# A four-block transformer stack on one core: left-over queries copied beside a segment's own, the output projection in halves of heads and columns, and a new table of order

## The chip, the cores and the metric

The kernel runs on one core of a Trainium2 chip. A core has five engines with instruction streams of their own: TensorE (PE in the profile; its weight loads are listed apart as PEld), VectorE (DVE), ScalarE (ACT), GpSimd (POOL) and SyncE (SP). They meet only through semaphores and share one on-chip memory; products land in eight accumulation banks (pb0 to pb7, 128 partitions by 512 floats), from which DVE or ACT must copy them out. The metric is the device time of one execution in microseconds; lower is better.

## The reference

`x` is 2048 tokens by 512. Four residual blocks follow each other: A, B, A, B, each on a layernorm of `x`.

```python
def _A_ref(x, mem0, Wq, Wk, Wv, Wo, seg_len):      # 32 heads of 128, M = 8 memory rows, seg_len = 32
    mem = mem0
    for s in range(n_seg):                          # 64 segments, one after the other
        h = concat([mem, x[32 rows of segment s]])  # 40 rows
        q, k, v = h @ Wq, h @ Wk, h @ Wv
        scores = where(mask, q @ k.T * scale, -1e9) # memory columns open to all, the rest causal
        o = softmax(scores) @ v @ Wo
        mem = o[:8]                                 # the next segment's memory
        outs.append(o[8:])

def _B_ref(x, wqkv, wo):                            # linear attention, 32 heads of 16
    pq, pk = phi(q), phi(k)                         # phi(t) = t+1 or exp(t), plus 1e-6
    kv = sum over tokens of pk^T v;  z = sum of pk
    o = (pq @ kv) / (pq . z + 1e-6);  return o @ wo
```

Block A is a recurrence over 64 segments: a segment's first eight output rows enter the next one's projections. Two A blocks make 128 such steps.

## The kernel before

**Rows.** A segment with its memory has 40 rows, but the column-tiled products take 32. So a block of 32 rows holds the eight memory rows (places 0 to 7) and the first 24 tokens (8 to 31). The left-over eight tokens of four segments form a fifth block of 32 rows, the left block, projected once for four segments (`prepare`, `left_block`). 128 tokens, four segments, are a tile; there are 16.

**A segment.** `project` (L721) multiplies a block with Wq, Wk and Wv. Four products of 32 output rows each go to the four 32-column groups of the array (`tile_position`), group j taking heads 8j to 8j+7; a run of 16 products fills a bank with half of the heads (half b = 0 or 1). Q and K are then turned: the bank is copied out (L572 on ACT, L573 on DVE), and half 0 is transposed by a DMA on SP's queue (L734), half 1 by TensorE (L741) and another copy. Results are `qT`, `kT`, and `qTl`, `kTl` of the left block.

**Memory attention** (`mem_attention`, L802 to L836) handles the eight memory queries: the products with left keys and own keys, exp, mask, sums, reciprocal by Ln and Exp, product with V, and a multiplication into `oTb`. **Own attention** (`x_attention`, L854 to L893) takes the 24 own queries and the eight left-over ones of the segment against the own keys: for each of the 32 heads one product with `qT[..., 8:32]` (24 columns, L854) and one with `qTl` (8 columns, L856), under the same keys. Its results are used one segment later.

**Output.** `out_proj` (L913) runs 32 products of 512 columns, column group j again holding heads 8j to 8j+7, so the bank holds four partial sums over heads in four row groups. Two copies of 256 columns bring it to `outW`. `next_mem` (L936) picks rows 0 to 7 and adds the four partial sums with `selm`, four products with `outW` as weights; a small copy puts the result into the next block. `residual` (L951, L956) picks the other rows with `selx` and `sell` as weights and 512 moving columns. `outW` and these selectors are 32-bit.

**Block B** is worked per tile of 128 tokens: `b_in` (L1045 to L1081) behind the A block's last rows, `b_mid` once, `b_out` (L1137, L1147) before the next A block's tile or at the end. Weights are loaded at the start: Wv, Wk and Wq by DMAs on ACT's queue, Wo in four parts and wqkv on SP's, and B's `wo` on POOL's.

**Order.** A planner (`_Prog`) sets each engine's order at build time. Every operation has a place (segment, name of its group, number in it); its priority is segment times `PERIOD` plus an entry of `OFFSET`, lower first, among what the planner's own costs make ready. `MODE_SLACK` says how long TensorE may prefer work of the same mode, column-tiled or whole array. The program that comes out is a fixed sequence for each engine with semaphore waits.

## Time and profile before

| | |
|---|---|
| median of three runs | 1967.08 us (1965.83 to 1967.78) |
| the profiled execution | 1967.05 us, span 1965.3 us |
| mean granted TensorE clock | 0.990 |
| busy: PE, ACT, DVE | 93%, 66%, 49% of the span |
| products and weight loads recorded | 39757 and 39837 |
| DMA | 96.31 MB |

The profile names a group of instructions by source line, engine, operation and tiles, with its count, the time in which at least one of them ran, the mean of one, and the engine's idle time just before them with what ended it. A product's duration contains the time in which it drains, during which the next one already runs; how far apart products start is therefore read from the starts in the timeline. Nearly all small tiles lie in one allocation, `arena_sb`.

### The profile page before, as it was taken

How to read it: one execution, taken by the hardware profiler on the slowest of the kernel's cores; microseconds unless marked ns; L12 is line 12 of the kernel's file. 1: busy time of each engine (PE TensorE's matmuls, PEld its weight loads, DVE VectorE, ACT ScalarE, POOL GpSimd, SP SyncE). 2: the span in 40 equal slices, each digit the busy share in tenths (PEclk: the TensorE clock that was granted, in tenths of full speed). 3: DMA queues.
4: the chain of work that ended last, by engine and by line, in shares of the span. 5: the costliest groups of instructions: out<-in, count | busy, mean ns of one | idle time of the engine just before them, and what ended most of it. 6: DMA issues, size and time to landing. Idle time of an engine off the chain costs nothing.

```text
span 1965.3 us, 86728 instructions
## 1 busy us (share of the span) xinstructions
PE 1836.8 (93%) x39757; PEld 1108.9 (56%) x39837; DVE 960.1 (49%) x2856; ACT 1295.4 (66%) x3170; POOL 74.5 (4%) x172
## 2 busy tenths in 40 slices
PE   2899999999999999999789999999999999999996
PEld 0455565556555655656445566555656556665652
DVE  1254455455445545454544455555455455555555
ACT  1566666666676766766456767666767777776765
POOL 2000000000000000000000000000000000000000
PEclk9899999999999999999899999999999999999999
DMA  8511222122112211211121211211122121222213
GB/s 307 123 32 35 40 38 43 32 38 38 38 35 37 43 32 42 34 40 35 28 43 27 40 40 40 38 35 43 35 40 46 33 43 38 40 38 41 55 35 118
DMA packets 228221, 96.31 MB, mean 49 GB/s; under 512 B 211624, under 2 KB 222000, under 8 KB 226320
## 3 DMA queue, kind: packets, MB, share of 16 engines
q1 hardware_dynamic: 220656, 62.58, 17.5%
q0 software_dynamic: 5616, 15.60, 2.6%
q10 hardware_dynamic: 1584, 12.58, 1.6%
q8 instruction: 311, 5.10, 1.1%
q14 instruction: 54, 0.44, 0.1%
HBM read 29.89 MB, written 10.49 MB: 21 GB/s over the span
## 4 chain that ended last, share of the span: by engine, by line
PE 80%; DMA 14%; ACT 3%; DVE 2%; issue 1%; ACTq 0%; SPq 0%; DVEq 0%
PE pb L721 33%; PE pb L913 15%; DMA arena_sb<-arena_sb 11%; PE pb L892 3%; PE pb L802 3%; PE pb L936 3%; PE pb L854 3%; PE pb L741 3%; PE pb L1045 3%; PE pb L819 2%; PE pb L951 2%; DMA Wq_sb<-in_A_Wq_dram 2%; ACT arena_sb L572 2%; PE pb L1081 1%; PE pb L833 1%; PE pb L832 1%
## 5 line engine op out<-in xcount | busy, mean ns | idle before, releaser
L572 ACT ACTIVATE arena_sb<-pb 128x512 bf16<-128x512 f32 (+5 forms) x1448 | 749.9, 525 | 385.5 <-PE pb L721 288.3
L721 PE MATMUL pb<-Wq_sb,arena_sb 128*32 128x512 bf16 x5120 | 342.8, 384 | 20.8 <-DMA Wq_sb<-in_A_Wq_dram 20.5
L721 PE MATMUL pb<-Wk_sb,arena_sb 128*32 128x512 bf16 x5120 | 339.2, 381 | 0.0
L721 PE MATMUL pb<-Wv_sb,arena_sb 128*32 128x512 bf16 x5120 | 330.1, 381 | 0.3 <-DVE arena_sb L573 0.3
L913 PE MATMUL pb<-Wo_sb,arena_sb 128*32 128x512 bf16 x5184 | 320.6, 384 | 3.7 <-DMA Wo_sb<-in_A_Wo_dram 2.8
L573 DVE COPY arena_sb<-pb 128x512 bf16<-128x512 bf16 (+2 forms) x356 | 123.1, 362 | 279.2 <-PE pb L741 275.2
L877 DVE TENSOR_TENSOR arena_sb<-arena_sb 32x256 bf16<-32x256 bf16 x512 | 212.7, 415 | 70.3 <-ACT arena_sb L873 58.4
L572 ACT ACTIVATE outW_sb<-pb 128x256 fp32r<-128x256 f32 x290 | 111.4, 384 | 162.7 <-PE pb L913 157.9
L721 PEld LDWEIGHTS pb<-Wv_sb,arena_sb 128*32 128x32 bf16 x5120 | 143.3, 97 | 133.5 <-issue 2.6
L721 PEld LDWEIGHTS pb<-Wk_sb,arena_sb 128*32 128x32 bf16 x5120 | 137.7, 97 | 134.5 <-issue 1.6
L721 PEld LDWEIGHTS pb<-Wq_sb,arena_sb 128*32 128x32 bf16 x5120 | 128.1, 97 | 146.8 <-DMA Wq_sb<-in_A_Wq_dram 20.8
L913 PEld LDWEIGHTS pb<-Wo_sb,arena_sb 128*32 128x32 bf16 x5184 | 138.2, 97 | 115.0 <-issue 5.9
L573 DVE CAST arena_sb<-pb 128x128 bf16<-128x128 f32 (+3 forms) x282 | 101.0, 358 | 202.7 <-PE pb L721 62.8
L892 PE MATMUL pb<-arena_sb 128*128 128x128 bf16 x1024 | 139.5, 218 | 5.1 <-DVE arena_sb L879 5.1
L893 PE MATMUL pb<-arena_sb 128*128 128x32 bf16 x1024 | 126.7, 179 | 0.0
L802 PE MATMUL pb<-arena_sb 128*128 128x32 bf16 x2016 | 108.0, 177 | 17.4 <-DMA arena_sb<-arena_sb 15.5
L809 ACT ACTIVATE arena_sb<-pb 128x256 bf16<-128x256 f32 x252 | 96.1, 382 | 38.7 <-PE pb L802 30.7
L879 DVE TENSOR_TENSOR arena_sb<-arena_sb 32x64 bf16<-32x64 bf16 x512 | 111.0, 217 | 15.8
L741 PE MATMUL pb<-id_sb,arena_sb 128*128 128x128 bf16 x1024 | 86.1, 221 | 25.3 <-ACT arena_sb L572 20.7
L741 PEld LDWEIGHTS pb<-id_sb,arena_sb 128*128 128x128 bf16 x1024 | 57.7, 98 | 86.2 <-ACT arena_sb L572 52.6
L802 PEld LDWEIGHTS pb<-arena_sb 128*128 128x128 bf16 x2016 | 84.4, 96 | 24.7 <-DMA arena_sb<-arena_sb 18.3
L892 PEld LDWEIGHTS pb<-arena_sb 128*128 128x128 bf16 x1024 | 91.3, 97 | 6.6 <-DVE arena_sb L879 5.7
(109 smaller groups left out, 2406.7 us busy)
## 6 DMA issues: line engine op xcount, KB each, us to landing
arena_sb<-arena_sb SPq DMA_TRANSPOSE x384, 2.5
Wv_sb<-in_A_Wv_dram ACTq DMA_DIRECT2D x1, 4096.0 KB, 15.0
Wk_sb<-in_A_Wk_dram ACTq DMA_DIRECT2D x1, 4096.0 KB, 24.9
Wq_sb<-in_A_Wq_dram ACTq DMA_DIRECT2D x1, 4096.0 KB, 34.2
Wo_sb<-in_A_Wo_dram SPq DMA_DIRECT2D x4, 1024.0 KB, 7.1
xs_scratch<-x_sb POOLq DMA_DIRECT2D x32, 128.0 KB, 2.0
pq_scratch<-arena_sb POOLq DMA_DIRECT2D x32, 128.0 KB, 3.1
x_sb<-xs_scratch POOLq DMA_DIRECT2D x16, 128.0 KB, 2.3
```

The costliest lines, as they stand in the source:

```text
L572: return e.activation(o() if callable(o) else o, i() if callable(i) else i, ACTF.Copy)
L573: return e.tensor_copy(o() if callable(o) else o, i() if callable(i) else i)
L721: r = pe.matmul(tl.f32()[32 * j:32 * j + 32, 0:512], blk[:, c, :], W[:, c, o:o + 512], start=(c == 0), stop=(c == 3), tile_position=(0, 32 ...
L741: r = pe.transpose(tt.bf16()[:, 128 * i:128 * i + 128], img[:, k, 128 * i:128 * i + 128], id_sb[:, :])
L802: r = pe.matmul(tl.f32()[:, o:o + 32], kk[:, hh, :, :].rearrange("p j x -> p (j x)"), qT[:, r2, hh, :, 0:8], start=True, stop=True)
L809: add("act", lambda a: a.activation(Pm[:, k, :, :].rearrange("p a q -> p (a q)"), tl.f32()[:, 0:256], ACTF.Exp, scale=SCALE), c_act(256), ...
L854: pe.matmul(tl.f32()[q, 32 * hh:32 * hh + 24], kT[:, r2, hh, j, :], qT[:, r2, hh, j, 8:32], start=True, stop=True, tile_position=(0, 32 * j))
L877: add("dve", lambda v, q=q, j=j: v.tensor_tensor(Pbx[q, :, j, 0:32], Px[q, :, :], Rx[q, :, :], ALU.mult), c_dve(256) + 0.075, reads=["Px", ...
L879: add("dve", lambda v, q=q, j=j: v.tensor_tensor(Pbx[q, :, j, 32:40], PLL[q, g2, :, gl], Rx[q, :, 24:32], ALU.mult), c_dve(64) + 0.075, re ...
L892: pe.matmul(o, vimg[:, r2, e], Pbx[:, hh, :, 0:32], start=True, stop=False)
L893: return pe.matmul(o[:, :, 24:32], vleft[:, g2, e], Pbx[:, hh, :, 32:40], start=False, stop=True)
L913: r = pe.matmul(tl.f32()[32 * j:32 * j + 32, :], oT[:, 4 * hh + j, :], Wo_sb[:, 8 * j + hh, :], start=(hh == 0), stop=(hh == 7), tile_posi ...
```

## The change

1. In `x_attention` the eight left-over queries of the segment are copied from `qTl` into `qT[..., 0:8]`, over the memory queries, one copy for each half of heads; then a single product of 32 columns per head takes the place of the 24 and 8. The left-over queries now stand at 0 to 7 instead of 24 to 31, and the slices behind follow (sums, multiplications, products with V, copies, and the mask `mx`).
2. In `out_proj` a column group holds half of the heads and half of the columns: 64 products of 256 columns. The bank then holds two partial sums of heads by two column halves in 256 columns. The two copies are 128 columns wide. `next_mem` has two products, each with a 16-column selector for both column halves; `residual` has two products of 256 columns with different selectors for one of 512.
3. The loads get places in the table (`ld0` to `ld4`), the load of B's `wo` waits until wqkv has landed, and the memory load is listed ahead of the first `x` load.
4. `OFFSET` is a new table, with groups of their own for the first and last tiles; `MODE_SLACK` goes from 25.37 to 26.39 and `LOOK` from 0.103 to 0.

```diff
-MODE_SLACK = 25.37
-LOOK = 0.103
+MODE_SLACK = 26.39
+LOOK = 0.000
...
+    "ld2": (20.70,),
+    "ld3": (4.75,),
+    "ld4": (-15.85,),
...
+    for i, (W, v, nm, t) in enumerate(((Wq_sb, qk_view[0], "Wq", 12.0), (Wk_sb, qk_view[1], "Wk", 21.0),
+                                       (Wv_sb, qk_view[2], "Wv", 30.3))):
+        P.at(-998 + i, "ld%d" % (2 + i))
+        late.append(add("act", lambda a, W=W, v=v: a.dma_start(W[:, :, :], v), 0.5, writes=[nm], dsem="d" + nm, lat=t))
...
     def load_wo_b(n):
-        add("pool", lambda e: e.dma_start(MB_sb[:, :, :], B_wo.rearrange("(c p) f -> p c f", p=128)), 1.1,
+        add("pool", lambda e: e.dma_start(MB_sb[:, :, :], B_wo.rearrange("(c p) f -> p c f", p=128)), 1.1, after=[late[-1]],
...
+            for b in range(2):
+                hs = slice(4 * b, 4 * b + 4)
+                evac(qT[:, r2, hs, :, 0:8], qTl[:, g2, hs, :, gl], 128, reads=[("qTl", g2, b)], writes=[("qT", r2, b)])
...
                         for j in range(4):
-                            q = slice(32 * j, 32 * j + 32)
-                            pe.matmul(tl.f32()[q, 32 * hh:32 * hh + 24], kT[:, r2, hh, j, :], qT[:, r2, hh, j, 8:32],
-                                      start=True, stop=True, tile_position=(0, 32 * j))
-                            r = pe.matmul(tl.f32()[q, 32 * hh + 24:32 * hh + 32], kT[:, r2, hh, j, :],
-                                          qTl[:, g2, hh, j, gl], start=True, stop=True, tile_position=(0, 32 * j))
+                            r = pe.matmul(tl.f32()[32 * j:32 * j + 32, 32 * hh:32 * hh + 32], kT[:, r2, hh, j, :],
+                                          qT[:, r2, hh, j, :], start=True, stop=True, tile_position=(0, 32 * j))
...
                 def mm(pe, hh=hh):
-                    for j in range(4):
-                        r = pe.matmul(tl.f32()[32 * j:32 * j + 32, :], oT[:, 4 * hh + j, :], Wo_sb[:, 8 * j + hh, :],
-                                      start=(hh == 0), stop=(hh == 7), tile_position=(0, 32 * j))
+                    for i in range(2):
+                        for j in range(4):
+                            k, d = divmod(j, 2)
+                            n = 2 * k + i
+                            r = pe.matmul(tl.f32()[32 * j:32 * j + 32, 0:256], oT[:, 4 * hh + n, :],
+                                          Wo_sb[:, 8 * n + hh, 256 * d:256 * d + 256], start=(hh == 0 and i == 0),
+                                          stop=(hh == 7 and i == 1), tile_position=(0, 32 * j))
...
-                cs = slice(256 * h, 256 * h + 256)
-                evac(outW[:, w, cs], lambda cs=cs: tl.f32()[:, cs], 256, tiles=[tl],
+                cs = slice(128 * h, 128 * h + 128)
+                evac(outW[:, w, cs], lambda cs=cs: tl.f32()[:, cs], 128, tiles=[tl],
...
-                    for c in (2 * h, 2 * h + 1):
-                        r = pe.matmul(tl.f32()[:, 8 * c:8 * c + 8], outW[:, w, 128 * c:128 * c + 128], selm_sb[:, :],
-                                      start=True, stop=True)
+                    return pe.matmul(tl.f32()[:, 16 * h:16 * h + 16], outW[:, w, 128 * h:128 * h + 128], selm_sb[:, :],
+                                     start=True, stop=True)
...
+            def pick(pe, sel, u, first, last):
+                for d in range(2):
+                    r = pe.matmul(tl.f32()[:, 256 * d:256 * d + 256], sel(d), outW[:, u, :], start=first and d == 0, stop=last,
+                                  skip_group_check=True)
+                return r
```

Since the table decides the order, three places of the built programs are shown. The first is ACT's stream at the start of the program, with the three large weight loads; before:

```order
L600 DMA Wv_sb<-in_A_Wv_dram 128x4x4096
L600 DMA Wk_sb<-in_A_Wk_dram 128x4x4096
L600 DMA Wq_sb<-in_A_Wq_dram 128x4x4096
L615 ACT_TABLE_LOAD
L572 ACTIVATE memT_sb<-pb 128x32
```

and in the changed program:

```order
L624 DMA Wv_sb<-in_A_Wv_dram 128x4x4096
L624 DMA Wk_sb<-in_A_Wk_dram 128x4x4096
L624 DMA Wq_sb<-in_A_Wq_dram 128x4x4096
L640 ACT_TABLE_LOAD
L591 ACTIVATE memT_sb<-pb 128x32
```

The three loads stand in the same order in both: V's weights first, Q's last.

The second place is TensorE's stream in the second segment of a tile (segment 17 of the first A block), from the projection of K's half 0, which a DMA turns, to the memory attention's products (L802, L834 after). Lines L721 and L753 are projections, L741 and L773 TensorE's transposes of half 1; the bank numbers are shown. Before:

```order
L721 MATMUL pb4<-Wk_sb,arena_sb 32x512 x16
L721 MATMUL pb1<-Wq_sb,arena_sb 32x512 x16
L721 MATMUL pb7<-Wv_sb,arena_sb 32x512 x16
L721 MATMUL pb2<-Wk_sb,arena_sb 32x512 x16
L721 MATMUL pb6<-Wv_sb,arena_sb 32x512 x16
L741 MATMUL pb5<-id_sb,arena_sb 128x128 x4
L741 MATMUL pb3<-id_sb,arena_sb 128x128 x4
L802 MATMUL pb4<-arena_sb 128x32 x8
```

and in the changed program:

```order
L753 MATMUL pb6<-Wk_sb,arena_sb 32x512 x16
L753 MATMUL pb1<-Wk_sb,arena_sb 32x512 x16
L753 MATMUL pb7<-Wq_sb,arena_sb 32x512 x16
L753 MATMUL pb4<-Wv_sb,arena_sb 32x512 x16
L753 MATMUL pb3<-Wv_sb,arena_sb 32x512 x16
L773 MATMUL pb2<-id_sb,arena_sb 128x128 x4
L834 MATMUL pb0<-arena_sb 128x32 x4
L773 MATMUL pb5<-id_sb,arena_sb 128x128 x4
L925 MATMUL pb6<-arena_sb 128x128
L926 MATMUL pb6<-arena_sb 128x4x8
```

Half 1 of Q and K now goes ahead of both projections of V, and the two transposes are set apart, with four memory products between them; a further pair of L925 and L926 with its like, four transposes of a layernorm and then the second four memory products (which wait for K's DMA) follow.

The third is TensorE's stream in the same kind of segment, from the output projection (L913, L949 after) to the next segment's first projection. L868 and L869 are the own attention's sums, L1045 and L1085 products of block B, L889 the own scores. Before:

```order
L913 MATMUL pb1<-Wo_sb,arena_sb 32x512 x32
L868 MATMUL pb3<-arena_sb,bo_sb 128x256
L869 MATMUL pb3<-arena_sb,bo_sb 128x8x8
L951 MATMUL pb0<-outW_sb,selx_sb 128x512
L956 MATMUL pb0<-outW_sb,sell_sb 128x512
L936 MATMUL pb4<-selm_sb,outW_sb 128x8 x4
L951 MATMUL pb2<-outW_sb,selx_sb 128x512
L721 MATMUL pb7<-Wq_sb,arena_sb 32x512 x16
```

and in the changed program:

```order
L949 MATMUL pb0<-Wo_sb,arena_sb 32x256 x64
L889 MATMUL pb4<-arena_sb 32x32 x32
L753 MATMUL pb2<-Wv_sb,arena_sb 32x512 x16
L753 MATMUL pb7<-Wq_sb,arena_sb 32x512 x16
L972 MATMUL pb1<-selm_sb,outW_sb 128x16 x2
L1085 MATMUL pb6<-arena_sb 128x512 x2
L901 MATMUL pb4<-arena_sb,bo_sb 128x256
L902 MATMUL pb4<-arena_sb,bo_sb 128x8x8
L753 MATMUL pb5<-Wq_sb,arena_sb 32x512 x16
```

The own scores now follow the output projection instead of going ahead of it, two projections of the left block stand between the output projection and the memory products, and B's products and the sums stand between these and the next projection. Over the whole program TensorE changes between column-tiled and whole-array products 586 times before and 654 times now.

133 lines of the change are left out of this document (77 added, 56 removed), and 8 rows, old and new, of the table OFFSET.

## The prediction

> **What bounds the kernel now.** I read the page's totals and slices first.
>
> ```profile
> span 1965.3 us, 86728 instructions
> PE 1836.8 (93%) x39757; PEld 1108.9 (56%) x39837; DVE 960.1 (49%) x2856; ACT 1295.4 (66%) x3170; POOL 74.5 (4%) x172
> PE   2899999999999999999789999999999999999996
> ```
>
> TensorE is busy from the second slice to the last, with one dip where the second A block begins. A busy PE may still be a waiting one, so the busy time by stages came next (columns: length, then busy time and count of each engine).
>
> ```profile
> 0.00:36.00 36.00, 1.48 (x12) 0.87 (x12) 4.95 (x11) 5.23 (x18) 11.83 (x54) 1.00 0.93 375
> 80.00:940.00 860.00, 835.45 (x18675) 511.67 (x18704) 424.09 (x1319) 587.78 (x1449) 24.46 (x45) 1.00 0.20 37
> 1025.00:1890.00 865.00, 841.84 (x18588) 514.07 (x18632) 443.68 (x1314) 602.15 (x1485) 30.62 (x56) 1.00 0.21 40
> ```
>
> The two long stages hold 1725 of the 1965 us, and TensorE idles in 24.5 and 23.2 us of them: 47.7 us, 2.8%. ACT works 68% and 70% of them, DVE 49% and 51%. The first 36 us are a different thing: DMA at 93%, TensorE nearly still. So in 88% of the span the sequence of products sets the time, and I price the change by how far apart products start. For that the timeline serves, since a duration contains the drain. (Columns: start, length, then what.)
>
> ```profile
> 1003.08 1.04 PE L913 MATMUL pb<-Wo_sb,arena_sb 128*32 128x512 bf16 x16
> 1003.94 1.04 PE L721 MATMUL pb<-Wv_sb,arena_sb 128*32 128x512 bf16 x16
> 1020.90 0.18 PE L893 MATMUL pb<-arena_sb 128*128 128x32 bf16 x1
> 1021.00 0.21 PE L854 MATMUL pb<-arena_sb 128*32 128x24 bf16 x4
> 1021.04 0.19 PE L856 MATMUL pb<-arena_sb 128*32 128x8 bf16 x4
> 1021.19 0.18 PE L856 MATMUL pb<-arena_sb 128*32 128x8 bf16 x4
> 1021.31 0.19 PE L832 MATMUL pb<-arena_sb 128*128 128x32 bf16 x1
> ```
>
> Sixteen products of 512 columns in four column groups take 0.86 us, 0.215 us for each four. Small column products go four at a time: from 1021.04 to 1021.19 are six steps of 0.025 us, with 24 columns or 8 alike. A change of mode shows at both ends: L893 to L854 takes 0.10 and L856 to L832 0.12 us, where the steps alone would be 0.025; I take 0.09 for a change.
>
> **The change part by part.** All sums start from the profiled execution's own 1967.05 us (span 1965.3 and 1.75 around it), which is 0.03 from the median.
>
> *Own scores.* There are 4096 L854 and 4096 L856 products, 64 a segment, so 16 steps a segment; half of them go. 8 steps x 128 segments x 0.025 = **-25.6 us**. That 32 columns cost a step like 24 is read from the left block's scores, the same product of 32:
>
> ```profile
> L768 PE MATMUL pb<-arena_sb 128*32 128x32 bf16 x1024 | 13.8, 177 | 2.4 <-DMA arena_sb<-arena_sb 2.4
> ```
>
> 177 ns each, where L854's mean is 179.
>
> *Memory rows.* Four L936 become two. They take 32-bit weights, and their loads come one by one:
>
> ```profile
> 1037.11 0.52 PEld L936 LDWEIGHTS pb<-selm_sb,outW_sb 128*128 128x128 f32 x4 [0.42 <-ACT outW_sb L572]
> 1037.71 0.19 PEld L951 LDWEIGHTS pb<-outW_sb,selx_sb 128*128 128x128 f32 x1
> ```
>
> One load lasts 0.19 us; four last 0.52, so they start (0.52 - 0.19) / 3 = 0.11 us apart. 504 products become 252: 252 x 0.11 = **-27.7 us**.
>
> *Residual.* One product of 512 columns becomes two of 256 under different 32-bit weights, 160 times. Does the second load hide behind the first product? A pair with such loads stands at a tile's end:
>
> ```profile
> 363.29 0.48 PE L951 MATMUL pb<-outW_sb,selx_sb 128*128 128x512 f32 x1
> 363.61 0.40 PE L956 MATMUL pb<-outW_sb,sell_sb 128*128 128x512 f32 x1
> 363.85 0.69 PE L936 MATMUL pb<-selm_sb,outW_sb 128*128 128x8 f32 x4
> ```
>
> The first takes 0.32 us (0.215 of columns and one exposed load of 0.11), the second 0.24: its load was nearly hidden. With 256 columns half of 0.215 falls away from each: 0.21 + 0.13 = 0.34 instead of 0.32, so 160 x 0.02 = **+3.2 us**. The bounds are 0 and a fully exposed second load, 160 x 0.11 = 17.6. The Trainium skill ("TensorE: Matmul & The Clock Gate", section "Part 3: Packing small matmuls — row/col tiling") states that a weight load overlaps a running product only when their row groups differ; all rows are used here, so by it the term would be near 17. The 0.24 us row goes against that, but it is one kind of place.
>
> *Output projection.* 5184 products, 1296 steps of 0.215 us, become 2592 steps of 256 columns. Half of 0.215 is 0.108; the only 256-column product here is a first of its burst:
>
> ```profile
> 1010.09 0.28 PE L868 MATMUL pb<-arena_sb,bo_sb 128*128 128x256 bf16 x1 [0.98 <-DVE arena_sb L862]
> 1010.21 0.19 PE L869 MATMUL pb<-arena_sb,bo_sb 128*128 128x64 bf16 x1
> ```
>
> 0.12 us to the next. The cost lies between 0 and 1296 x (0.24 - 0.215) = 32 us. I take 0.109, near the half, because the steps run in long rows and four small loads fit into 0.025 us above: 1296 x 0.003 = **+4 us**.
>
> *Changes of mode.* 586 become 654: 68 x 0.09 = **+6.1 us**.
>
> *Copies and evacuations.* 256 copies of 128x128 come in (by the order 192 on DVE, 64 on ACT), and 324 copies of the output projection shrink from 256 columns (384 ns on ACT) to 128 (288 ns). No copy in on-chip memory of that size is in the trace; the nearest is DVE's of 128x128 16-bit from a bank, 0.23 us, so about 44 us on DVE. It has room, and the order puts the first copy just ahead of the memory attention's mask, where DVE waits anyway:
>
> ```profile
> 372.56 0.29 DVE L811 TENSOR_TENSOR arena_sb<-arena_sb 128x256 bf16<-128x256 bf16 x1 [0.81 <-ACT arena_sb L809]
> 372.82 0.23 DVE L573 COPY arena_sb<-pb 128x128 bf16<-128x128 bf16 x1
> ```
>
> 0.81 us of idle hold a 0.23 us copy. **0 us**; uncovered, at 0.23 x 256, it is 59. The quicker evacuation shortens the way from L913 to L936, but TensorE stood idle for it for 1.5 and 1.0 us only in the two stages (below): 0.
>
> *Loads.* The order shows that the Q, K, V loads are **not** reordered: V, K, Q, as before, Q's landing last.
>
> ```profile
> Wv_sb<-in_A_Wv_dram ACTq DMA_DIRECT2D x1, 4096.0 KB, 15.0
> Wk_sb<-in_A_Wk_dram ACTq DMA_DIRECT2D x1, 4096.0 KB, 24.9
> Wq_sb<-in_A_Wq_dram ACTq DMA_DIRECT2D x1, 4096.0 KB, 34.2
> arena_sb<-in_B_wo_dram POOLq DMA_DIRECT2D x1, 512.0 KB, 9.9
> ```
>
> ```profile
> PE pb L721 <- DMA Wq_sb<-in_A_Wq_dram: 20.5, 1, 20.5
> ```
>
> TensorE's first projection follows Q's landing after 20.5 us of waiting. What does move is B's wo: its 0.52 MB leave this window, at 375 GB/s (the row of the first 36 us) **-1.4 us**. On POOL's queue the load now waits for wqkv; behind it stand the first tile's move to scratch and the third x load, tens of microseconds later in their need. On SP's queue the parts of Wo stand between the same DMA transposes as before.
>
> *Order.* What TensorE waits for in the two stages is mostly two things (first window, then second):
>
> ```profile
> L802 PE MATMUL pb<-arena_sb 128*128 128x32 bf16 x976 | 52.0, 177 | 7.0 <-DMA arena_sb<-arena_sb 6.1
> L741 PE MATMUL pb<-id_sb,arena_sb 128*128 128x128 bf16 x488 | 41.4, 221 | 14.2 <-ACT arena_sb L572 11.1 <-DVE arena_sb L573 3.0
> L936 PE MATMUL pb<-selm_sb,outW_sb 128*128 128x8 f32 x244 | 40.2, 252 | 1.5 <-ACT outW_sb L572 1.0
> ...
> L802 PE MATMUL pb<-arena_sb 128*128 128x32 bf16 x960 | 51.9, 177 | 8.1 <-DMA arena_sb<-arena_sb 7.1
> L741 PE MATMUL pb<-id_sb,arena_sb 128*128 128x128 bf16 x480 | 40.1, 221 | 9.7 <-ACT arena_sb L572 8.2 <-DVE arena_sb L573 1.3
> L936 PE MATMUL pb<-selm_sb,outW_sb 128*128 128x8 f32 x243 | 39.3, 256 | 1.0 <-ACT outW_sb L572 0.5
> ```
>
> L741 idles 23.9 us in them, mostly for the copy of its projection.
>
> ```profile
> 1002.22 1.04 PE L721 MATMUL pb<-Wk_sb,arena_sb 128*32 128x512 bf16 x16
> 1003.30 0.60 ACT L572 ACTIVATE arena_sb<-pb 128x512 bf16<-128x512 f32 x1 [0.27 <-PE pb L721]
> ```
>
> The run of K starts at 1002.22, the next run at 1003.08 (above), ACT's copy of K at 1003.30 and it lasts 0.60, so K can be turned 0.82 us after the next run's start, if ACT was free. Before, one run of V (0.86 us) lay between K's half 1 and its transposes: a tight fit. Now two lie between, 1.72 us. The DMA's 15.1 us ahead of L802 I leave: four runs followed K's half 0 before, and four do now. Of the 23.9 I take half, because more of the 512-column copies go to DVE now (691 ns there, 597 on ACT), and what TensorE no longer waits for here it may meet at the next product: **-12 us**, with bounds of -39 (both waits gone) and +20 (shorter work covers the same chains less).
>
> **Sum:** 1967.05 - 25.6 - 27.7 + 3.2 + 4 + 6.1 - 1.4 - 12 = 1913.65, say **1914 us**, 2.7% faster.
>
> **The rivals.**
>
> *Exposed loads.* If the second selector's load does not hide, 1914 + 14 = 1928; if the 256-column steps also cost 0.12, another 28: 1956. For it: 32-bit loads are serial at L936. Against: 363.61 to 363.85.
>
> *Waits in place of work.* TensorE's removed work was cover for chains through ACT and DVE: after the memory products come exp, mask, sums, Ln, Exp and a multiplication. If the waits grow by 20 us instead of falling by 12: 1946. For it: small pieces of projections, four products at a time, now stand between the memory products in the new order, each with two changes of mode. Against: ACT and DVE idle 30% and 49% of the long stages, so their chains need not queue.
>
> *The copies hold up the recurrence (slower).* The copy overwrites memory queries, so it must wait until both memory products of its half have read them, and on DVE it stands ahead of the mask on which the sums, the output projection and the next segment's memory depend. If both halves' copies came to lie on that way, at 0.23 each, 0.46 x 128 = 59 us: 1973. It decides from 53 / 128 = 0.41 us a segment. Against: the 0.81 us gap.
>
> *A fuller order.* If both waits above go, 39 instead of 12: 1887.
>
> *The change doesn't do what it says* holds for the loads, as shown, and is in the sum: reordering would bear on the 20 us that TensorE waits for Q's weights, and I give nothing for it.
>
> **How the numbers follow.** Forecast 0.58 (1903 to 1930 by its own terms), exposed loads 0.13, waits 0.14, fuller order 0.10, slower copies 0.05. The range leaves out the slower case, the upper half of the exposed loads and the last part of the fuller order: 1893 to 1946. A difference within 0.2% (3.9 us) could not be told from none. Faster takes all but the last case and a rest of the exposed loads: 0.93; same 0.02; slower 0.05.
>
> **What would show it.** The own scores' line has 4096 products; memory rows 252 with about the same 0.11 between loads; L741's successor idles less than 23.9 us in the long stages; the output projection's runs of 32 take about 0.87 us (0.96 would be the dear case); the two residual products start some 0.21 us apart and the next follows after 0.13; the first projection starts 1.4 us earlier. Wrong it is if idle before the memory attention's sums or masks grows, or if copies of 128x128 in `arena_sb` end TensorE's waits.

## The result, and the profile after

The changed kernel takes 1910.07 us (median of four runs, 1903.94 to 1912.49); the kernel before, beside it, 1967.43 us. The ratio is 0.9701, with a 95% interval of 0.9674 to 0.9728: 2.9% faster, where 1914 us and 2.7% were forecast. The profiled execution took 1909.38 us, 57.7 less than that of before; the sum said 53.4 less.

First the page of the changed kernel, its totals, and then the busy time by stages (length; busy time and count of PE, PEld, DVE, ACT, POOL; clock, DMA share, GB/s).

```profile
span 1907.5 us, 88958 instructions
PE 1780.8 (93%) x40739; PEld 1192.9 (63%) x40833; DVE 1092.2 (57%) x3242; ACT 1162.2 (61%) x3040; POOL 74.8 (4%) x172
```

```profile
0.00:36.00 36.00, 2.57 (x24) 1.33 (x28) 5.19 (x12) 4.96 (x17) 11.29 (x53) 1.00 0.89 361
...
80.00:920.00 840.00, 820.21 (x19211) 554.69 (x19244) 493.65 (x1504) 530.16 (x1405) 24.98 (x46) 1.00 0.20 38
1000.00:1840.00 840.00, 815.51 (x19166) 557.63 (x19218) 509.17 (x1522) 539.51 (x1422) 30.63 (x56) 1.00 0.21 41
```

TensorE is as full as before: it idles 19.8 and 24.5 us in the long stages, 44.3 together, where it was 47.7. Over the whole span its busy time fell by 56.0 us (1836.8 to 1780.8) and its idle time by 1.8. So nearly all of the gain is work that is gone from TensorE's sequence. What it waits for has changed, though. These are the groups of the two stages, in the first window and then in the second:

```profile
L834 PE MATMUL pb<-arena_sb 128*128 128x32 bf16 x976 | 54.7, 177 | 8.4 <-DMA arena_sb<-arena_sb 8.2
L773 PE MATMUL pb<-id_sb,arena_sb 128*128 128x128 bf16 x488 | 45.5, 220 | 3.1 <-DVE arena_sb L592 1.9 <-ACT arena_sb L591 1.2
L800 PE MATMUL pb<-arena_sb 128*32 128x32 bf16 x480 | 7.0, 178 | 3.8 <-DMA arena_sb<-arena_sb 3.8
...
L834 PE MATMUL pb<-arena_sb 128*128 128x32 bf16 x976 | 54.2, 177 | 9.8 <-DMA arena_sb<-arena_sb 9.8
L773 PE MATMUL pb<-id_sb,arena_sb 128*128 128x128 bf16 x488 | 45.8, 220 | 3.8 <-DVE arena_sb L592 1.9 <-ACT arena_sb L591 1.7
L800 PE MATMUL pb<-arena_sb 128*32 128x32 bf16 x480 | 6.7, 177 | 3.1 <-DMA arena_sb<-arena_sb 3.1
```

The transposes (L773, before L741) idle 6.9 us where it was 23.9. The products behind the DMA transposes (L834, before L802) idle 18.2 where it was 15.1, and the left block's scores (L800, before L768) 6.9, where it was 0.7 (2.4 in the whole run). The wait for the copies went, as the order let one expect: 17.0 us less. More than half of that, 9.3 us, came back at the products behind the DMA, and 5.5 ahead of the memory sums (L851) and of block B's products (L1085).

The timeline shows what the shorter sequence looks like. (Start, length to the last end, line and tiles, count.)

```profile
995.11 1.93 PE L949 MATMUL pb<-Wo_sb,arena_sb 128*32 128x256 bf16 x64
996.87 0.82 PE L753 MATMUL pb<-Wq_sb,arena_sb 128*32 128x512 bf16 x12
997.62 0.28 PE L972 MATMUL pb<-selm_sb,outW_sb 128*128 128x16 f32 x1
997.75 0.28 PE L901 MATMUL pb<-arena_sb,bo_sb 128*128 128x256 bf16 x1
997.87 0.19 PE L902 MATMUL pb<-arena_sb,bo_sb 128*128 128x64 bf16 x1
997.90 0.26 PE L972 MATMUL pb<-selm_sb,outW_sb 128*128 128x16 f32 x1
998.01 0.48 PE L990 MATMUL pb<-outW_sb,selx_sb 128*128 128x256 f32 x2
998.44 1.05 PE L753 MATMUL pb<-Wq_sb,arena_sb 128*32 128x512 bf16 x16
...
1007.16 0.38 PE L889 MATMUL pb<-arena_sb 128*32 128x32 bf16 x32
1007.40 1.93 PE L949 MATMUL pb<-Wo_sb,arena_sb 128*32 128x256 bf16 x64
```

A run of 64 halves of the output projection takes 1.76 us to the next start, the 32 own scores 0.24, a memory product 0.11 to 0.13, and the two residual products with the change of mode behind them 0.43.

### The profile page after: what moved, and what is told of

Read it like the earlier page. It is cut to its first block, busy times and chain, and to the rows that moved or that the text cites. A ratio compares the mean times of both kernels' runs of the same rounds, so it can differ in the third digit from the quotient of the medians.

```text
span 1907.5 us, 88958 instructions
## 1 busy us (share of the span) xinstructions
PE 1780.8 (93%) x40739; PEld 1192.9 (63%) x40833; DVE 1092.2 (57%) x3242; ACT 1162.2 (61%) x3040; POOL 74.8 (4%) x172
## 3 DMA queue, kind: packets, MB, share of 16 engines
q1 hardware_dynamic: 220656, 62.58, 18.2%
## 4 chain that ended last, share of the span: by engine, by line
PE 76%; DMA 16%; DVE 4%; ACT 3%; issue 1%; SPq 0%; ACTq 0%; DVEq 0%
PE pb L753 34%; PE pb L949 16%; DMA arena_sb<-arena_sb 13%; PE pb L1085 3%; PE pb L925 3%; PE pb L990 3%; PE pb L773 2%; PE pb L834 2%; ACT arena_sb L591 2%; PE pb L851 2%; PE pb L972 2%; PE pb L889 2%; DMA Wq_sb<-in_A_Wq_dram 2%; DVE arena_sb L592 2%; PE pb L1121 1%; PE pb L865 1%
## 5 line engine op out<-in xcount | busy, mean ns | idle before, releaser
L591 ACT ACTIVATE arena_sb<-pb 128x512 bf16<-128x512 f32 (+6 forms) x1287 | 667.3, 526 | 389.3 <-PE pb L753 326.0
L592 DVE CAST arena_sb<-pb 128x512 bf16<-128x512 f32 (+3 forms) x534 | 242.2, 456 | 353.9 <-PE pb L972 176.7
L753 PE MATMUL pb<-Wq_sb,arena_sb 128*32 128x512 bf16 x5120 | 354.0, 384 | 23.3 <-DMA Wq_sb<-in_A_Wq_dram 20.9
L753 PE MATMUL pb<-Wv_sb,arena_sb 128*32 128x512 bf16 x5120 | 318.7, 381 | 0.1
L949 PE MATMUL pb<-Wo_sb,arena_sb 128*32 128x256 bf16 x10368 | 314.5, 276 | 2.4 <-DVE arena_sb L868 1.8
L753 PE MATMUL pb<-Wk_sb,arena_sb 128*32 128x512 bf16 x5120 | 314.0, 380 | 0.0
L949 PEld LDWEIGHTS pb<-Wo_sb,arena_sb 128*32 128x32 bf16 x10368 | 269.8, 98 | 33.5 <-DVE arena_sb L868 22.8
L753 PEld LDWEIGHTS pb<-Wk_sb,arena_sb 128*32 128x32 bf16 x5120 | 138.7, 97 | 131.7 <-issue 1.2
L753 PEld LDWEIGHTS pb<-Wv_sb,arena_sb 128*32 128x32 bf16 x5120 | 138.5, 97 | 123.2 <-issue 1.8
L753 PEld LDWEIGHTS pb<-Wq_sb,arena_sb 128*32 128x32 bf16 x5120 | 123.5, 97 | 137.9 <-DMA Wq_sb<-in_A_Wq_dram 21.1
L591 ACT ACTIVATE outW_sb<-pb 128x128 fp32r<-128x128 f32 x257 | 71.4, 278 | 194.6 <-PE pb L949 191.6
L592 DVE COPY arena_sb<-pb 128x512 bf16<-128x512 bf16 (+2 forms) x265 | 97.7, 371 | 100.5 <-PE pb L773 77.7
L925 PE MATMUL pb<-arena_sb 128*128 128x128 bf16 x1024 | 128.6, 217 | 5.6 <-DVE arena_sb L912 5.5
L834 PE MATMUL pb<-arena_sb 128*128 128x32 bf16 x2016 | 112.5, 177 | 22.1 <-DMA arena_sb<-arena_sb 21.2
L926 PE MATMUL pb<-arena_sb 128*128 128x32 bf16 x1024 | 118.1, 178 | 0.0
L868 DVE TENSOR_TENSOR arena_sb<-pb,arena_sb 128x128 bf16<-128x128 f32 x252 | 72.0, 290 | 64.8 <-ACT arena_sb L856 37.3
L834 PEld LDWEIGHTS pb<-arena_sb 128*128 128x128 bf16 x2016 | 86.9, 96 | 29.8 <-DMA arena_sb<-arena_sb 24.9
L773 PE MATMUL pb<-id_sb,arena_sb 128*128 128x128 bf16 x1024 | 95.7, 220 | 10.0 <-DVE arena_sb L592 5.6
L773 PEld LDWEIGHTS pb<-id_sb,arena_sb 128*128 128x128 bf16 x1024 | 58.4, 97 | 67.4 <-issue 30.1
```

The costliest lines, as they stand in the source:

```text
L591: return e.activation(o() if callable(o) else o, i() if callable(i) else i, ACTF.Copy)
L592: return e.tensor_copy(o() if callable(o) else o, i() if callable(i) else i)
L753: r = pe.matmul(tl.f32()[32 * j:32 * j + 32, 0:512], blk[:, c, :], W[:, c, o:o + 512], start=(c == 0), stop=(c == 3), tile_position=(0, 32 ...
L773: r = pe.transpose(tt.bf16()[:, 128 * i:128 * i + 128], img[:, k, 128 * i:128 * i + 128], id_sb[:, :])
L834: r = pe.matmul(tl.f32()[:, o:o + 32], kk[:, hh, :, :].rearrange("p j x -> p (j x)"), qT[:, r2, hh, :, 0:8], start=True, stop=True)
L868: add("dve", lambda v: v.tensor_tensor(oTb[:, s % NO, 16 * b:16 * b + 16, 0:8], pv.f32()[:, 0:128].rearrange("p (n q) -> p n q", q=8), Rm[ ...
```

## The experiments

Every kernel ran beside the kernel before on the same chip: 1970.44 us in the first four, 1971.38 in the next four, 1968.67 and 1967.69 in the last two pairs.

**The changed kernel again**, as the measure for the others.

> The changed kernel, unaltered, as the measure for the runs beside it. Both theories: about 1910 us, 0.970 of the kernel before.

1913.8 us (1908.69 to 1916.91), ratio 0.971 [0.9687, 0.9734]: the same as the first time. Its profiled execution took 1916.45 us, 7 more than the first one, and idles 47.6 us in the two long stages, where that had 44.3. So a difference of a few us between two profiles tells little.

**Own scores in 24 and 8 columns again**, in the changed kernel's order:

```diff
-    r = pe.matmul(tl.f32()[..., 32 * hh:32 * hh + 32], kT[...], qT[:, r2, hh, j, :], ...)
+    pe.matmul(tl.f32()[..., 32 * hh + 8:32 * hh + 32], kT[...], qT[:, r2, hh, j, 8:32], ...)
+    r = pe.matmul(tl.f32()[..., 32 * hh:32 * hh + 8], kT[...], qT[:, r2, hh, j, 0:8], ...)
```

> The changed kernel with its order untouched, but each own score of 32 columns is issued as two, 24 and 8, from the same copied tile (4096 products more, 1024 steps of four). Theory 'work' (TensorE's own steps set the time): 1024 x 0.025 = 25.6 us slower than the changed kernel beside it, about 1936. Rival 'order' (the gain comes from the new table, and shorter products only make room for waits): less than 8 us slower.

1953.35 us, ratio 0.9908 [0.9891, 0.9925]: 39.5 us more than the changed kernel, not 25.6. The timeline of this kernel tells why; a run of 64 begins in groups of four and then falls into ones:

```profile
1025.24 0.21 PE L890 MATMUL pb<-arena_sb 128*32 128x24 bf16 x4
1025.28 0.19 PE L892 MATMUL pb<-arena_sb 128*32 128x8 bf16 x4
...
1025.46 0.17 PE L890 MATMUL pb<-arena_sb 128*32 128x24 bf16 x1
1025.48 0.17 PE L892 MATMUL pb<-arena_sb 128*32 128x8 bf16 x1
...
1025.76 1.94 PE L952 MATMUL pb<-Wo_sb,arena_sb 128*32 128x256 bf16 x64
```

The first 32 products take 0.22 us (1025.24 to 1025.46), 0.028 for each four; the last 32 take 0.30, 0.037 for each four. So the half that the change removes is the dear half: 0.52 us in place of 0.24 (1007.16 to 1007.40 above), 0.28 x 128 = 36 us. Added up over whole traces, from each first start to the next other product's, the own scores take 72.5 us here, 33.1 in the changed kernel and 69.5 in the kernel before: 39.4 us more for this run, as its time says, and 36.4 for the change itself.

**Four memory products of eight columns again**, in the same order; `outW` and the rest as changed:

```diff
-    return pe.matmul(tl.f32()[:, 16 * h:16 * h + 16], outW[:, w, 128 * h:128 * h + 128], selm_sb[:, :], ...)
+    for d in range(2):
+        r = pe.matmul(tl.f32()[:, 16 * h + 8 * d:16 * h + 8 * d + 8], outW[:, w, 128 * h:128 * h + 128],
+                      selm_sb[:, 8 * d:8 * d + 8], ...)
```

> The changed kernel with its order untouched, but each of the two 16-column memory products is issued as two of 8 columns under the same weights (252 products and 32-bit loads more). Theory 'work': 252 x 0.11 = 27.7 us slower, about 1938. Rival 'order': less than 8 us slower, since other work stands behind the memory products anyway.

1931.22 us, ratio 0.9799 [0.9778, 0.9821]: 17.4 us more, between the two theories. The rows give the full price:

```profile
1013.05 0.39 PE L973 MATMUL pb<-selm_sb,outW_sb 128*128 128x8 f32 x2
1013.29 0.28 PE L901 MATMUL pb<-arena_sb,bo_sb 128*128 128x256 bf16 x1
```

Two products take 0.24 us to the next start where one took 0.13. Added up over all runs of these products in the trace, from each first start to the next other product's, it is 66.9 us here and 39.6 in the changed kernel: 27.3, against 27.7 expected. Some 10 us of that did not reach the end.

**The output projection in 512 columns again**, in the same order, with everything behind it as changed. Of the bank only 256 columns go on, so half of the sum is left out.

```diff
-    for i in range(2):
-        for j in range(4):
-            ... 64 products of 256 columns
+    for j in range(4):
+        ... 32 products of 512 columns: Wo_sb[:, 8 * j + hh, :]
```

> The changed kernel with its order untouched, but the output projection issues 32 products of 512 columns, column group j with all columns of heads 8j to 8j+7, in place of 64 of 256; the later steps still read 256 columns, so half of the columns of the partial sums is left out and the output is not the reference's. Theory 'work' with a 256-column step at 0.109: 4 us faster than the changed kernel (0 if the step is half of 0.215). Rival 'dear steps' at 0.12: 28 to 32 us faster.

1902.71 us, ratio 0.9654 [0.9634, 0.9674]: 11 us less, more than the 4 and far from the 28. The row of a run:

```profile
991.96 1.91 PE L946 MATMUL pb<-Wo_sb,arena_sb 128*32 128x512 bf16 x32
993.70 0.82 PE L753 MATMUL pb<-Wq_sb,arena_sb 128*32 128x512 bf16 x12
```

1.74 us, against 1.76 for 64 halves. By the medians of such runs (1.734 before, 1.757 after) it is 0.023 x 162 = 3.7 us. Added up over the whole trace, the runs take 290.0 us here and 295.5 in the changed kernel, 5.5 more. The other half of the 11 us I can't place; the four executions of the changed kernel beside it lie 8 us apart, so part of it may be noise.

**The loads in the order Q, K, V**, which the change's words promise and its table undoes:

```diff
-    "ld2": (20.70,),
-    "ld3": (4.75,),
-    "ld4": (-15.85,),
+    "ld2": (0.00,),
+    "ld3": (0.00,),
+    "ld4": (0.00,),
```

> The changed kernel with the three table entries of the weight loads set to zero, so that they are issued Q, K, V, as the change's name says; the planner's order of products stays nearly the same (the difference lies in the first rows). Theory (TensorE's first 128 products are of Q and K only, 8 runs of 0.86 us, and all of them waited for Q's landing as the last at 33.0 us; with Q at about 13, K at 23 and V at 33 they lie inside the load window): 7 us less, plus 1 to 4 us of the transposes behind them, so 8 to 11 us faster than the changed kernel, some 1904 us. Rival (V's and the output weights' landing gate the first segment just the same, and the chain of the first segment, not the products, fills the time behind them): within 2 us of the changed kernel, 1912 to 1916.

1904.86 us (1903.02 to 1907.18), ratio 0.9664 [0.9649, 0.9678]: 9 us less than the changed kernel by the ratios, as the theory had it, and the fastest complete kernel here. Landings from the DMA view and TensorE's waits, of this kernel:

```profile
Wq_sb<-in_A_Wq_dram ACTq DMA_DIRECT2D x1, 4096.0 KB, 13.7
Wk_sb<-in_A_Wk_dram ACTq DMA_DIRECT2D x1, 4096.0 KB, 23.7
Wv_sb<-in_A_Wv_dram ACTq DMA_DIRECT2D x1, 4096.0 KB, 34.4
```

```profile
PE pb L773 <- ACT arena_sb L591: 10.3, 11, 7.0
...
PE pb L753 <- DMA Wk_sb<-in_A_Wk_dram: 5.5, 1, 5.5
```

The wait for Q's weights, 20.9 us in the changed kernel, is gone. A wait of 5.5 for K and one of 7.0 for a copy of the first segment stand in its place; 20.9 - 5.5 - 7.0 = 8.4. Not all of this is seen further on: the first output projection starts at 59.2 us, where it was 64.9 and 64.0 in the two profiles of the changed kernel. TensorE's granted clock is lower in between (0.88 in the first 36 us and 0.79 from there to 80 us, where the changed kernel's first profile has 1.00 and 0.89). Where the rest of the 9 us comes from is open.

**Both changes of products under the old table.** This is the kernel before with parts 1 and 2 of the change (the copies and 32-column scores, the output projection in halves) and everything else left; in the old table two entries for the copies were added ahead of the others of `x`:

```diff
-    "x": (2.30, -1.40, 0.00, -0.90, 12.00, ...
+    "x": (2.20, 2.20, 2.30, -1.40, 0.00, -0.90, 12.00, ...
```

> The kernel before with both changes of products (32-column own scores with the copies; output projection in halves) but with the table of order and the loads of before. The planner's rules on that give 812 changes of mode (654 in the changed kernel, 586 before). Theory (the products' own lengths give 36 + 17.5 - 11 - 1 = 41 us, as the runs so far measured them one by one, and the 226 more changes of mode take 0.09 us each, 20 us): 1970 - 41 + 20 = about 1949 us. Rival A (the table does nothing by itself, and mode changes hide): about 1928. Rival B (without a new table the shorter products uncover the waits for the transposes' copies and for the DMA transposes, 20 us and more on top): 1965 or more.

1972.31 us, ratio 1.001 [0.9999, 1.0021]: **no gain at all**. Rival B's number is right. The windows of before, in this kernel:

```profile
80.00:940.00 860.00, 826.77 (x19029) 542.71 (x19066) 428.41 (x1387) 575.21 (x1499) 24.45 (x45) 1.00 0.20 37
...
1025.00:1890.00 865.00, 831.76 (x18970) 545.13 (x19023) 451.03 (x1426) 576.02 (x1489) 30.62 (x56) 1.00 0.20 40
```

TensorE idles 33.2 + 33.2 = 66.4 us, 18.7 more than before, and there are 812 changes of mode in place of 586; at 0.09 us each these make 20 us, an estimate. So work was saved, and as much was lost again, about half of it in changes of mode and half in waits. The waits are not where rival B put them: ahead of the transposes (L746) they fell from 23.9 to 12.5 us in the two windows, and behind the DMA transposes (L807) they rose only from 15.1 to 18.3. The new ones are ahead of the memory sums (L824) and of the products that pick the memory rows (L945), where the whole run had 1.8 and 3.0 us before:

```profile
L824 PE MATMUL pb<-arena_sb,one_sb 128*128 128x128 bf16 x504 | 69.5, 220 | 10.5 <-DVE arena_sb L816 6.9
...
L945 PE MATMUL pb<-selm_sb,outW_sb 128*128 128x16 f32 x252 | 55.4, 270 | 14.3 <-ACT outW_sb L572 8.0 <-DVE outW_sb L573 5.2
```

The sums wait for DVE's mask, and what DVE did just before the mask was, in 10.0 of these 10.5 us, a copy out of a bank; a copy of left-over queries it was in 0.1. So the two entries that were added for these copies are not what holds up the sums. Other entries for them were not tried, and other places of the order may depend on them.

**The old products under the new table**: the changed kernel with parts 1 and 2 of the change undone, and the entries of the copies taken out of the table:

```diff
-    "x": (3.45, 13.20, 11.25, -10.75, ...
+    "x": (11.25, -10.75, ...
-    "xL": (12.95, 3.75, 2.20, 1.30, ...
+    "xL": (2.20, 1.30, ...
```

> The changed kernel with both changes of products undone (24 and 8 columns, 512-column output projection), under the new table (less the two entries of each row that belong to the copies): 796 changes of mode. Theory (the table's worth is one of order and holds for both kinds of products; 142 more changes of mode than the changed kernel at 0.09 us, 13 us): 1914 + 36 + 17.5 - 11 - 1 + 13 = about 1968 us, level with the kernel before. Rival (the table fits the new products only; under the old ones the waits it took away come back and others with them): 1985 us or more.

2086.96 us, ratio 1.0589 [1.0569, 1.0608]: 116 us slower than before, far over the theory. Not all of this is waiting: TensorE's granted clock was 0.977 to 0.979 in the four executions of this kernel, where the kernel before has 0.987 to 0.992 beside it. By these shares some 20 to 25 us of the 116 go to the clock, an estimate. **One product undone at a time** then tells whether the table is bound to one of them; first the scores (the table as just shown), then the output projection (the table untouched), each with the order planned anew.

```diff
-    r = pe.matmul(tl.f32()[32 * j:32 * j + 32, 32 * hh:32 * hh + 32], ...)          # the first kernel
+    pe.matmul(..., qT[:, r2, hh, j, 8:32], ...)
+    r = pe.matmul(..., qTl[:, g2, hh, j, gl], ...)
...
-    for i in range(2):                                                              # the second kernel
-        for j in range(4):
+    for j in range(4):
+        r = pe.matmul(tl.f32()[32 * j:32 * j + 32, :], oT[:, 4 * hh + j, :], Wo_sb[:, 8 * j + hh, :], ...)
```

> The changed kernel with only the own scores undone (24 and 8 columns, no copies) and the order planned anew under the new table: 708 changes of mode (654). With the order of the changed kernel held fixed the same scores took 1953 us. Theory (the table is bound to the output projection in halves, not to the scores, so planning anew does no harm here): 1953 to 1965 us. Rival (any change of a product's length under a fixed table throws the order off): 2000 us or more, and then the 2087 us of both products undone come from the scores.

> The changed kernel with only the output projection undone (512 columns, four memory products, one residual product) and the order planned anew under the new table: 856 changes of mode. Theory (as in the run before it: here the order breaks, with TensorE waiting ahead of the output projection for the memory attention's multiplication): 2040 us or more. Rival (the two undone products only add up, 1914 + 17.5 - 11 - 1): 1915 to 1940 us.

2031.68 us, ratio 1.0321 [1.0301, 1.0342], and 2001.43 us, ratio 1.0164 [1.0146, 1.0182]. Either breaks it. The first answers the rival, the second fell between the two numbers, but is nearer to a broken order than to a sum. The first can be set beside the run with scores of 24 and 8 columns in the *fixed* order, 1953 us: the same numbers and sizes of products, 78 us apart. Apart from the order, the two differ in the copies, which the slower one does without. The long stages in that fixed order, then in the order planned anew:

```profile
80.00:930.00 850.00, 829.24 (x20869) 565.91 (x20896) 488.43 (x1483) 525.39 (x1386) 24.37 (x45) 1.00 0.21 38
1020.00:1870.00 850.00, 824.74 (x20741) 567.21 (x20788) 500.49 (x1492) 529.47 (x1399) 30.57 (x56) 1.00 0.21 40
```

```profile
80.00:960.00 880.00, 833.97 (x20813) 563.75 (x20847) 467.19 (x1371) 518.63 (x1370) 24.38 (x45) 1.00 0.19 36
1050.00:1930.00 880.00, 823.99 (x20470) 558.04 (x20516) 466.58 (x1352) 530.21 (x1380) 30.01 (x55) 0.99 0.20 39
```

46 us of idle against 102. And the largest of these waits is at the same place in the broken orders: ahead of the output projection, for the multiplication that ends the memory attention (L868 in the first, L863 in the second and third: `tensor_tensor` with `Rm` into `oTb`). In turn the changed kernel, the old scores, the old projection, and both:

```profile
L949 PE MATMUL pb<-Wo_sb,arena_sb 128*32 128x256 bf16 x10368 | 314.5, 276 | 2.4 <-DVE arena_sb L868 1.8 <-DMA Wo_sb<-in_A_Wo_dram 0.3
```

```profile
PE pb L948 <- DVE arena_sb L868: 35.3, 41, 1.4
PE pb L924 <- DVE arena_sb L911: 21.4, 23, 3.7
```

```profile
PE pb L941 <- DVE arena_sb L863: 41.8, 65, 0.9
```

```profile
L940 PE MATMUL pb<-Wo_sb,arena_sb 128*32 128x512 bf16 x5184 | 319.7, 387 | 34.0 <-DVE arena_sb L863 32.0
```

1.8 us of waiting for it in the changed kernel, 32 to 42 in the others. Here the four corners together, in us (the last corner from both measurements of the changed kernel):

| | products of before | one undone | changed products |
|---|---|---|---|
| table of before | 1971 | | 1972 |
| new table | 2087 | 2032 and 2001 | 1910 to 1914 |

**The copies cut to two columns of one head index**, the rest of each copy left out, in the same order:

```diff
-    evac(qT[:, r2, hs, :, 0:8], qTl[:, g2, hs, :, gl], 128, ...)
+    evac(qT[:, r2, hs, 0:1, 0:2], qTl[:, g2, hs, 0:1, 8 * g:8 * g + 2], 128, ...)
```

> The changed kernel in exactly its order, but each of the 256 copies of left-over queries moves 2 columns of one head in place of 128, so that it lasts some 0.06 us on DVE in place of 0.19 (what is left out: most of the copying; the own scores then multiply other numbers). Theory (copies lie in DVE's and ACT's idle time): within 3 us of the changed kernel, 1911 to 1917. Rival (the copies stand in the way of the mask and of the chain of the next segment): 0.13 us for each of the 256 at most, so up to 33 us less; anything from 8 us on speaks for it.

1911.87 us, ratio 0.9697 [0.9682, 0.9711]: as the theory said, but the run tells less than was meant. The copy on DVE in the changed kernel, and in this one:

```profile
L592 DVE COPY arena_sb<-arena_sb 128x128 bf16<-128x128 bf16 x192 | 36.8, 192 | 20.4 <-PE pb L834 18.9
```

```profile
L592 DVE COPY arena_sb<-arena_sb 128x8 bf16<-128x8 bf16 x192 | 32.4, 169 | 17.2 <-PE pb L834 15.3
```

A sixteenth of the elements still takes 169 of the 192 ns, so only 4 us of DVE's time went. That the copies cost next to nothing rests on other rows. The own scores, which alone read the copies, never find TensorE waiting. And the copies hardly hold up DVE's mask of the memory attention (L843, L811 before). Added up over its 252 places, the mask starts 24.1 us after the end of ACT's exp, where it was 9.3 (33 ns at each place are there at the least, 8.3 in all); of this, 14.1 us are at places where DVE comes straight from a copy out of a bank, and 0.5 where it comes from a copy of left-over queries.

```profile
L889 PE MATMUL pb<-arena_sb 128*32 128x32 bf16 x4096 | 50.6, 178 | 0.0
```

**Two more changes of mode in each segment**: one whole-array product between the two halves of the own scores, its columns read by nobody.

```diff
+    if b:
+        pe.matmul(tl.f32()[:, 256:288], kT[:, r2, 4, :, :], qT[:, r2, 4, 0, :], start=True, stop=True)
     for hh in range(4 * b, 4 * b + 4):
```

> The changed kernel in its order, with one whole-array product of 32 columns put between the first 16 and the last 16 own-score products of each segment, into columns of the bank that nobody reads: 128 products and 256 changes of mode more (910 for 654). Theory (a change takes 0.09 us each way, as read at two places of the trace of before): 256 x 0.09 + 128 x 0.025 = 26 us more than the changed kernel, 1938 to 1941. Rival (a change costs that only where the products on its two sides differ in length or in weights, or it is swallowed by waits that are there anyway): less than half, under 1927.

1916.27 us, ratio 0.9732 [0.9713, 0.9751]: 4 us more than the changed kernel by the ratios. And yet the price is right:

```profile
1005.41 0.28 PE L891 MATMUL pb<-arena_sb 128*32 128x32 bf16 x16
1005.62 0.19 PE L888 MATMUL pb<-arena_sb 128*128 128x32 bf16 x1
1005.74 0.28 PE L891 MATMUL pb<-arena_sb 128*32 128x32 bf16 x16
```

From the last score before it to the new product it is 0.108 us (median of 128), and 0.120 from there to the next score, each 0.09 over a step. In all the runs of own scores take 58.2 us where they took 33.1: 25.1 us more on TensorE's own time. Where they went shows in the two long stages:

```profile
80.00:920.00 840.00, 819.54 (x19018) 552.02 (x19016) 486.30 (x1481) 522.73 (x1386) 24.38 (x45) 1.00 0.20 38
1000.00:1840.00 840.00, 831.27 (x19329) 563.79 (x19325) 511.69 (x1518) 540.08 (x1428) 30.55 (x56) 1.00 0.22 41
```

In the first, TensorE idles 20.5 us, as in the changed kernel (19.8); in the second it idles 8.7, where that has 24.5. The same shows in how long the two A blocks take, from the first start of an output projection's product to the last, in us. Beside it stand the two other runs that add products to the fixed order, with half of what the additions take on TensorE's own time:

| | half of the addition | first A block | second A block |
|---|---|---|---|
| changed kernel, two profiles | | 874.1 and 875.3 | 887.5 and 890.8 |
| scores in 24 and 8 | 19.7 | 894.4 | 910.9 |
| four memory products | 13.7 | 890.8 | 894.0 |
| two more changes of mode | 12.6 | 886.9 | 883.5 |

The first block pays for each addition in full. In the second block the scores are paid in full as well, the memory products for less than half, and with the changes of mode it even becomes shorter: waits behind the DMA transposes and ahead of TensorE's transposes went (16.7 us in its window in the changed kernel, 5.6 here). Why the second block differs is not shown.

**The old table with more slack**: as the run with the new products and the old table, with two constants changed. The order has 738 changes of mode; the 682 in the expectation was a wrong count.

```diff
-MODE_SLACK = 25.37
-LOOK = 0.103
+MODE_SLACK = 40
+LOOK = 0.0
```

> The kernel before with both changes of products and the table of before, as in the run with the old table (1972 us), but MODE_SLACK at 40 in place of 25.37 and LOOK at 0: TensorE stays longer with work of one mode, and there are 682 changes of mode instead of 812. Theory (of the 41 us that the products gave, 20 went into changes of mode and about 19 into waits): 130 x 0.09 = 12 us less, about 1960 us, waits as they were. Rival (staying in a mode makes the recurrence wait instead, which is why the slack was 25): 1970 us or more, with more idle time of TensorE in the long stages than the 66 us of the run with the old table.

2045.22 us, ratio 1.0393 [1.037, 1.0416]. Fewer changes of mode, and 73 us slower than with the old constants: the rival is right, and TensorE idles 119.6 us in the long stages in place of 66.4. Which of the two constants does it is not shown. The products that pick the memory rows now find 26.1 us of idle ahead of them, mostly for ACT's copy of the output:

```profile
L945 PE MATMUL pb<-selm_sb,outW_sb 128*128 128x16 f32 x252 | 60.0, 272 | 26.1 <-ACT outW_sb L572 17.7 <-DVE outW_sb L573 7.2
```

## Why the prediction was right, step by step

The forecast of 1914 us holds, and its mechanism, less work in TensorE's sequence, is what the trace shows. But two terms were mis-sized by about 10 us each, in opposite directions. That the sum came out within 4 us is in part luck.

- **Own scores, -25.6: mis-sized, -36 by the rows; the run that undoes it says 39.5.** The count was right (4096 products). The step of 0.025 us was read in a run of 32, where 118 of the 128 segments had runs of 64, and their second half goes at 0.037.
- **Memory rows, -27.7: -27.3 on TensorE's own time, -17.4 by the run.** The 0.11 between loads is right. Undone, it was paid in full in the first A block and for less than half in the second.
- **Residual, +3.2: about +4.2.** Where one product became two, next to nothing: to the next whole-array product it is 0.319 us before (median of 58 places) and 0.319 or 0.325 after (30 and 28 places), and to the next projection 0.428 before (median of 38) and 0.41 to 0.44 after (21 places). The rows of one such place before:

```profile
1037.73 0.48 PE L951 MATMUL pb<-outW_sb,selx_sb 128*128 128x512 f32 x1
1038.14 1.05 PE L721 MATMUL pb<-Wq_sb,arena_sb 128*32 128x512 bf16 x16
```

  This is 0.41 us; after, 998.01 to 998.44 above is 0.43. The difference is far less than the 0.11 of a load that lies open, so the second 32-bit load is hidden. At a tile's end, where two became four, it is about 0.14 more, 30 times, 4.2 us: 0.55 before (median of 28 places, to a product that picks memory rows); after, 0.797 (30 places) to a projection, 0.69 without the 0.11 (0.428 less 0.319) by which a projection follows later. As the two are followed by different products, this is an estimate. The Trainium skill ("TensorE: Matmul & The Clock Gate", section "Part 3: Packing small matmuls — row/col tiling"), by whose rule the second load would have lain open for some 17 us (an estimate, 160 loads of 0.11 us), does not agree with these rows when its sentence on row groups is read alone; the same section also has the load pulled ahead into a background weight buffer, and that reading fits.
- **Output projection, +4: 3.7 by the medians, 5.5 by all runs of the trace, 11 by the run.** The steps of 256 columns are near their half; 5 us or more of the run's difference stay open.
- **Changes of mode, +6.1.** The price of 0.09 us is right. The run that added 256 shows that TensorE's time and the kernel's time are two things: 25 us became 4, though the first A block paid its half in full. The 68 of the change may have cost 1 us as well as 6. The Trainium skill ("TensorEngine Tiling (Array Packing)", section "Tiling Modes") states that changing the mode drains TensorE; it gives no time, and the rows here give 0.108 and 0.120 us from start to start.
- **B's wo, -1.4: -1.2.** Q's weights land 33.0 us after their issue, where it was 34.2:

```profile
Wq_sb<-in_A_Wq_dram ACTq DMA_DIRECT2D x1, 4096.0 KB, 33.0
```

  That the three loads keep their order was right. That nothing was given for a true reordering was no error of the forecast, but 9 us lay there.
- **Copies, 0.** The rows bear it out, though the run on them could not measure it. The reason that the prediction gave was weak: the gap of 0.81 us ahead of the mask was one place, and over all 252 places DVE idled 32.4 us there before, 0.13 at a place, less than one copy. The one sign named for "wrong", more idle ahead of the memory sums, came in small: 1.8 us before, 5.3 after (L851), over the whole run. DVE's copies out of the banks stand ahead of the mask there, more than those of left-over queries.
- **Order, -12: mis-sized, -3.4 in the first profile and -0.1 in the second.** The wait at the transposes fell by 17 us of the 23.9, more than the half that was assumed; "what TensorE no longer waits for here it may meet at the next product" then took nearly all of it. Over half came back at the DMA transposes, whose 15.1 us the prediction had left as they were, and at the left block's scores.

By the rows: -36 - 27.3 + 4.2 + 3.7 + 6.1 - 1.2 - 3.4 = -53.9, of 57.7 measured. The 3.8 us between them are less than the 7 by which two profiles of the changed kernel differ.

What the prediction had wrong in kind is the place of the order in the sum. It stood there as one small term beside the products. The corners show that it isn't a term: the same products give 0 under the old table and 57 with the new one, and the new table on the old products costs 116. The rival of waits in place of work (1946) was held unlikely because ACT and DVE have room; under the old table 18.7 us of waits came in just so, beside the changes of mode (1972 us in all), with ACT and DVE about as full as before (64% and 50% of the span). The new table keeps both away. It decided whether the lighter products pay, and the forecast did not see how much hung on it: it had read three places of the new order, and they do not show that the whole holds. That the new table fits the new products was in the change, and for the forecast it was luck.

## What to carry to other kernels

When a planner orders a kernel by a table of numbers, a changed product and the table are one change: a new product tried under the old table measures the table (here 0 of 57 us), and a changed product is best tried with the order held fixed. A price read from start to start is what an instruction takes on its engine; the kernel may pay all, two thirds or little of it (39.5 for 39.4, 17.4 for 27.3, 4 for 25 us here). Look at the stages one by one: here the first A block paid in full each time, and only the second gave something back. And read such a price in runs as long as most of those that go away.

## What was unexpected

- A long run of small column-tiled products slows down: 0.028 us for each four in the first 32, 0.037 in the next 32. With 32 products in a run it does not come to that: in the changed kernel every step but the first takes 0.025, in the second half of the heads too. What slows the long run is not shown.
- A change of mode costs TensorE 0.09 us each way; 25 us of it moved the end by about 4, as the second of the two A blocks became shorter.
- DVE's copy within on-chip memory takes 169 ns for 8 elements in a partition and 192 ns for 128.
- An order planned with more slack, and without the planner's look ahead, cost far more than the changes that it saved: 738 changes in place of 812, and 73 us more.
